# A fourth usual pair in the first gated block, statistics of later blocks made in its pairs, and rows split a pair later

## The chip, the cores and the metric

The kernel runs on one core of one Trainium2 chip. The metric is device time in microseconds (us), the median over several runs. The engines are PE (TensorE: matrix products, with its weight loads listed as PEld), DVE (VectorE), ACT (ScalarE), POOL (GpSimd) and SP (SyncE, which here only issues DMAs). Each engine takes its instructions in the order in which the program gives them.

## The reference

Four layers in a row on x of shape (1, 2048, 448), all in float32: attention, gated, attention, gated. Both attention layers share their weights, and so do both gated ones.

```python
def A(x, wqkv, wo):                      # 16 heads of 28
    q, k, v = heads_of(x @ wqkv)
    return merged(softmax(q @ k.T * 28 ** -0.5) @ v) @ wo
def B(x, w_gate, w_up, w_down):          # F = 1792
    return (sigmoid(x @ w_gate) * (x @ w_up)) @ w_down
x = x + A(layernorm(x)); x = x + B(layernorm(x))
x = x + A(layernorm(x)); x = x + B(layernorm(x))
```

## The kernel before

**Stages.** The program is written as one long order by hand: what is recorded first on an engine runs first there. A layer here means one attention layer and the gated layer after it, so there are two. Each goes through the projection (`project`), the attention (`attend`), the output projection (`out_project`) and the gated part (`gated`). x stays in SBUF all the time.

**Precision.** Matrix operands are kept as a high and a low float16 part, and a product is made of three matmuls (high-high, low-high, high-low). An ACT copy makes the high part, a DVE subtraction the low one.

**Attention.** Scores for three key tiles at a time go to three PSUM banks, and one ACT instruction (L1144) takes the exponential of all three. `FEW` says how many of a head's 64 units (a key tile by a block of queries) are taken out of this and done on DVE instead, in ten operations (L1154 to L1163, `score_aside`); the counts hold for layer 0 alone, layer 1 uses three in every head. While layer 0's attention runs, DVE and POOL also prepare the gated weights (`Prepare`): sums and splits, packed and written to DRAM.

**The gated part.** 2048 rows are four blocks b of 512 rows, and the 1792 features are seven pairs p of 256. "b1p4" is block 1, pair 4. `gate_and_up` makes one pair for one block. It uses a scheme with seven products instead of eight for 2x2 blocked matrices (Strassen's, in Winograd's form): `first`, `second`, `third` are chains whose PSUM bank ACT copies out (L1527), `c11_c22`, `c21` and `c12` complete the four quarters. DVE adds the bank `side` to the copies (L1543 after `c11_c22`, L1550 after `c12`). `c12` writes into the same `side` bank that L1543 reads. Then come the sigmoid (ACT, L1554) and the product (DVE, L1557). The order of PE in a pair is fixed: `first`, `apart`, `second`, `apart`, `third`, `c11_c22`, `c21`, `c12`, each for gate and up, at six or five matmuls of 256 columns a time.

**Down projection.** For most pairs it too has seven products: `Operands.early` and `late` make sums on DVE, `parts` and `rest` split them into `hparts` in the next pair, and while block b runs its gate and up, PE makes the products (`pieces`, L1454) of block b-1, one product k a pair, over all the pairs of that block; `finish` adds the result to x (L1472). The first `USUAL` pairs of block 0 do it the usual way instead: `split` makes one float16 pair a tile (L210, L211), and `down` runs 24 matmuls of 448 columns (L1502 to L1504) into four banks, one pair later. `add_usual(j)` adds bank j to x.

**The rest beside it.** `at[0]` to `at[5]` are lists of work recorded at six places of a pair: after `first`, `second`, `third`, `c11_c22`, the first sigmoids and products, and the end. `portions(b, p)` says how many steps of the next block's preparation are recorded at which of them. A block's 18 steps are: four `norm` (statistics of one tile of 128 rows: DVE L279 and L280, POOL L283 and L285), four `squares` (scaling L288 and a transpose L305 into `xs`), one step that stores `xs` to DRAM (SP, L317) and gathers it turned into `raw` (SP, L325 and L327), and nine that split it (`r11`, `t1`, `t2`, `t3`, `r21`, `t4`, `r22`, `last_low`, `last_rows`; DVE L371, L387, L390 and ACT L379, L381, L394).

**Slots.** Large tiles (`xn`, `xs`, `xraw`, `gu`, `dn` and others) share 19 slots of SBUF, handed out first freed, first used. When a pair is done, its two `gu` tiles (the gate weights and the up weights of a pair) are freed, and POOL issues the loads for the pair after next into the two slots that have been free longest (`used_gu`, L1345); products' weights `dn` follow (L1357). A load waits until the former holder of its slot is done, and everything behind it in POOL's queue waits too.

Of the kernel before, what the change touches and what calls it, by code (L numbers as in the profile page):

```python
# [11 lines left out]
F32 = mybir.dt.float32  # L12
BF16 = mybir.dt.bfloat16
F16 = mybir.dt.float16
# [5 lines left out]
P = 128  # L20
# [6 lines left out]
NB = 4  # L27
TB = NT // NB
# [8 lines left out]
NP = NF // 2  # L37
# [18 lines left out]

N_SUMS = 25
DN = D // 2
N_DN = 8
USUAL = 3  # L60
SHORT = ((10, 23, 12), (11, 24, 13), (8, 22, 9))

ASIDE = {1: ((6, 15, 1),), 2: ((4, 10, 3), (9, 15, 1)), 3: ((4, 9, 3), (8, 13, 1), (12, 15, 2))}
FEW = "2221212111111233"


TAIL = (0, 1, 3, 2, 5, 4, 6)
# [41 lines left out]
def interleaved_layers(ctx: ExitStack, tc: tile.TileContext, x_in, wqkv, wo, w_gate, w_up,  # L111
# [4 lines left out]
    cpool = ctx.enter_context(tc.tile_pool(name="cpool", bufs=1))  # L116
# [3 lines left out]
    big = Slots(spool, "s", N_SLOTS)  # L120
    qrt = Slots(spool, "q", N_QUART)
    uid = [0]
# [132 lines left out]
    class Block:  # L255
# [15 lines left out]
        def norm(self, js=range(TB)):  # L271
            b = self.b
            if js[0] == 0:
                uid[0] += 1
                self.mv = cpool.tile([P, TB, 2], F32, name=f"mv_{uid[0]}", tag="mv", bufs=2)
                self.rs = cpool.tile([P, TB], F32, name=f"rs_{uid[0]}", tag="rs", bufs=2)
            for j in js:
                st = cpool.tile([P, 6], F32, name=f"st_{uid[0]}_{j}", tag="st", bufs=4)
                nc.vector.bn_stats(st, x[:, b * TB + j, :])  # L279
                nc.vector.bn_aggr(self.mv[:, j, :], st)  # L280
            c = slice(js[0], js[-1] + 1)
            rs = self.rs[:, c]
            nc.gpsimd.tensor_scalar(rs, self.mv[:, c, 1], EPS, XS ** -2, op0=ALU.add,  # L283
                                    op1=ALU.mult)
            nc.gpsimd.tensor_tensor(rs, rs, nhalf[:, c], op=ALU.pow)  # L285
# [166 lines left out]

        def begin(self):
            uid[0] += 1
            self.mv = cpool.tile([P, TB, 2], F32, name=f"mv_{uid[0]}", tag="mv", bufs=2)
            self.rs = cpool.tile([P, TB], F32, name=f"rs_{uid[0]}", tag="rs", bufs=2)
            self.xn = big.get("xn", [P, TB, D])

        def stats(self, j):
# [103 lines left out]
    gu_parts = dpool.tile([NP, 2, P, N_SUMS, P], F16, name="gu_parts")  # L563
    dn_parts = dpool.tile([N_DN, P, NP, 2, DN], F16, name="dn_parts")

# [346 lines left out]
    class Prepare:  # L912
# [127 lines left out]
        def split(self, raw, kind, j):  # L1040
# [287 lines left out]
    class WeightsGated:  # L1328
# [24 lines left out]
                    nc.sync.dma_start(self.usual[p // 2][:, p % 2, i], dn_parts[k, :, p])  # L1353

        def load_dn(self, queue=nc.sync):
            self.dn.append(big.get("dn", [P, NP, 2, DN], F16))
            queue.dma_start(self.dn[-1], dn_parts[self.products.popleft()])  # L1357

        def used_gu(self):
            big.put(*self.gu.popleft())  # L1360
# [8 lines left out]
    def gated(layer, first, wt, before_next):  # L1369
        last = layer == LAYERS - 1  # L1370
# [1 line left out]
        low, high = slice(0, W // 2), slice(W // 2, W)  # L1372

        seq = [(b, p) for b in range(NB) for p in range(NP)]
        blks = [first]
        steps = deque()
        banks_of = {}


# [127 lines left out]
        def add_usual(j):  # L1507
            v = x[:, j, :]
            pm = accs[j].rearrange("p c n -> p (c n)")
            nc.vector.scalar_tensor_tensor(v, pm, back[:, 2:3], v, op0=ALU.mult, op1=ALU.add)  # L1510
# [95 lines left out]
        pend = []  # L1606
        for b, p in seq:
            if p == 0:
                if b + 1 < NB:
                    blks.append(Block(b + 1, True))  # L1610
                    steps.extend(blks[b + 1].steps())
                elif not last:
                    after = [Block(0), Block(1)]
                    blks.append(after[0])
                    steps.extend(after[0].steps())
                    ready = [steps.pop() for _ in range(2)]
                    squared = after[1].squared()
                    steps.extend(squared[:TB] + ready[::-1] + squared[TB:] +
                                 [after[1].store, after[1].gather])
            at = [[] for _ in range(6)]  # L1620

            if made:
                at[0].append(made.parts)
                at[1].append(made.rest)
            if done:
                at[1].append(lambda done=done: finish(*done))
                done = None
            for i, n in enumerate(portions(b, p)):
                at[i].append(lambda n=n: run_fill(steps, n))
            if b == 0 and p > USUAL or b == 1 and p == 0:  # L1630
                for j in range(TB)[p - USUAL - 1:p - USUAL] if b == 0 else range(
                        NP - USUAL - 1, TB):
                    at[0].append(lambda j=j: add_usual(j))


            if b > 0:
                some = [q for q in (0, 1, 6, 2, 3, 4, 5) if q in of_block(b - 1)]
                for q in some:
# [24 lines left out]

        b = NB - 1
# [10 lines left out]
        for k in TAIL[3:]:  # L1675
            if k == 6:
                for j, i in enumerate((0, 2)):
# [4 lines left out]
                    if last:  # L1682
                        t = b * TB + j
# [10 lines left out]
    def portions(b, p):  # L1694

        if b == 0:
            steps = {0: {1: 4, 5: 5}, 2: {1: 1, 2: 1, 3: 1, 5: 1}, 3: {1: 1, 2: 1, 3: 1, 5: 1},
                     4: {1: 1}}
        elif b < NB - 1:
            steps = {0: {1: 2, 2: 1}, 1: {1: 2, 2: 1}, 2: {1: 1, 2: 2}, 3: {5: 1},  # L1700
                     4: {1: 1, 3: 1}, 5: {1: 1, 3: 1}, 6: {1: 1, 2: 1, 3: 1, 5: 1}}
        else:
            steps = {0: {1: 2, 2: 1}, 1: {1: 2, 2: 1}, 2: {1: 1, 2: 2}, 3: {1: 2, 2: 2},
                     4: {1: 1, 2: 1}, 5: {1: 1, 2: 1}, 6: {1: 1, 2: 2, 5: 1}}
        return [steps.get(p, {}).get(i, 0) for i in range(6)]
# [6 lines left out]
    first = Block(0)  # L1712
# [81 lines left out]
```

## Time and profile before

| what | value |
|---|---|
| device time, median of 3 runs | 1914.47 us |
| lowest and highest | 1913.83, 1914.67 us |
| the profiled execution | 1918.24 us |
| its span, first to last instruction | 1916.4 us |
| PE busy | 1897.9 us (99%) |
| DVE busy | 1412.8 us (74%) |
| ACT busy | 1366.0 us (71%) |
| POOL busy | 240.6 us (13%) |
| granted PE clock, mean | 0.997 |

A row of the timeline gives the start in us from the span's start, the length, the engine, the line of the kernel, the operation with what it writes and reads, and how many such were merged; in brackets stands how long the engine sat idle before it and what ended that. A row of the windows view gives a stretch, its length, and for each engine the busy time in it with the number of instructions, then the mean granted clock of PE as a share of full speed. The page counts a matmul from its issue to its modelled end, and matmuls overlap, so that PE's busy time says when PE was not idle and not how fast it was.

### The profile page before, as it was taken

The numbers are of one execution on the slowest core, as the hardware profiler recorded it, in microseconds if no ns is written. First come the engines' busy times: TensorE is split into PE (matmuls) and PEld (weight loads), VectorE is DVE, ScalarE is ACT, GpSimd is POOL, SyncE is SP. The second block draws the span as 40 slices with busy tenths as digits, with TensorE's granted clock in tenths as the row PEclk, the third lists the DMA queues.
The fourth block names the chain that finished last, engine by engine and source line by source line (L and its number), as shares of the span: only waits on it lengthen the run. The fifth ranks groups of instructions, "written<-read, shape, count | busy, mean of one in ns | idle before, by whom it ended". The sixth has DMA issues, their size and how long they took to land. (4 is left out here: it accounts for less than half of the span.)

```text
span 1916.4 us, 56353 instructions
## 1 busy us (share of the span) xinstructions
PE 1897.9 (99%) x24317; PEld 1405.8 (73%) x24317; DVE 1412.8 (74%) x2816; ACT 1366.0 (71%) x1742; POOL 240.6 (13%) x467
## 2 busy tenths in 40 slices
PE   9999999999999999999999999999999999999999
PEld 4455655555566798999954568778888777899998
DVE  7648798687877598788663487778778667887764
ACT  5569999999983455454344799999999645555541
POOL 2013312232001111212100000000000011211110
PEclk9999999999999999999999999999999999999999
DMA  5575555345313657656634312122111235665752
GB/s 173 165 207 162 155 157 149 117 144 149 92 62 92 235 189 263 219 221 236 232 94 132 89 51 51 28 51 51 41 37 66 75 98 215 216 270 198 270 204 90
DMA packets 107298, 275.20 MB, mean 144 GB/s; under 512 B 12766, under 2 KB 63086, under 8 KB 106912
## 3 DMA queue, kind: packets, MB, share of 16 engines
q0 software_dynamic: 33088, 165.74, 24.5%
q1 hardware_dynamic: 73616, 105.54, 19.3%
q8 instruction: 192, 3.15, 0.7%
q14 instruction: 66, 0.54, 0.1%
q10 hardware_dynamic: 336, 0.23, 0.0%
HBM read 213.39 MB, written 50.73 MB: 138 GB/s over the span
## 5 line engine op out<-in xcount | busy, mean ns | idle before, releaser
L1144 ACT ACTIVATE prob_s<-sc 128x1536 f32<-128x1536 f32 x659 | 892.7, 1484 | 6.7 <-PE sc L1129 3.3
L1180 PE MATMUL acc<-prob_s,val_s 128*32 128x256 f32 (+3 forms) x7754 | 590.1, 383 | 0.0
L1129 PE MATMUL sc<-qp_s 114*32 114x512 f16 x7896 | 575.8, 379 | 0.0
L545 PEld LDWEIGHTS <-gu_s 128*128 128x128 f16 x4368 | 428.0, 98 | 60.3 <-issue 8.1
L1129 PEld LDWEIGHTS <-qp_s 114*32 114x32 f16 x8192 | 309.9, 96 | 176.3 <-issue 78.2
L1180 PEld LDWEIGHTS acc<-prob_s,val_s 128*32 128x32 f32 x7754 | 317.9, 110 | 100.8 <-issue 7.6
L545 PE MATMUL chain<-xwide_s,gu_s 128*128 128x256 f16 x2016 | 249.0, 273 | 4.1 <-DMA gu_s<-gu_parts 4.0
L1454 PE MATMUL dnp<-dn_s,hparts_s 128*128 128x224 f16 x2100 | 235.5, 259 | 0.0
L1454 PEld LDWEIGHTS <-hparts_s 128*128 128x128 f16 x2100 | 202.1, 98 | 4.8
L1527 ACT COPY one_q<-chain 128x256 f32<-128x256 f32 x224 | 82.0, 372 | 132.0 <-PE chain L545 131.3
L1160 DVE SCALAR_TENSOR_TENSOR power_q<-power_q,expo_q 128x512 f32<-128x512 f32 x222 | 153.7, 692 | 7.6
L545 PE MATMUL side<-xshort_s,gu_s 128*128 128x256 f16 x1120 | 142.1, 274 | 3.0 <-DVE one_q L1543 2.7
L530 PE MATMUL qkp<-xhl_s,wqk_s 128*128 128x512 f16 x616 | 138.0, 379 | 0.7 <-DVE xhl_s L509 0.3
L1543 DVE TENSOR_TENSOR one_q<-side,one_q 128x512 f32<-128x512 f32 x112 | 72.0, 684 | 83.4 <-PE side L545 83.4
L530 PEld LDWEIGHTS <-wqk_s 128*128 128x128 f16 x616 | 60.0, 98 | 70.1 <-ACT wqk_s L223 1.0
L1209 DVE STREAM_TRANSPOSE oturned_q<-acc 128x512 f32<-128x512 f32 x32 | 22.9, 717 | 118.4 <-PE acc L1180 118.4
L1345 POOL DMA_DIRECT2D gu_s<-gu_parts x104 | 56.0, 540 | 365.7 <-PE side L545 183.3
L545 PE MATMUL side<-xwide_s,gu_s 128*128 128x256 f16 x672 | 92.3, 274 | 0.0
L1407 ACT CAST hparts_s<-hsums_q 128x256 f16<-128x256 f32 (+1 forms) x144 | 68.4, 489 | 33.1 <-DVE hsums_q L1419 20.6
L722 ACT ACTIVATE qkhl_q<-qkp 128x512 f16<-128x512 f32 x56 | 33.2, 593 | 75.0 <-PE qkp L530 71.6
L1180 PE MATMUL acc<-power_q,val_s 128*32 128x256 f32 (+3 forms) x278 | 86.4, 393 | 0.0
L1554 ACT ACTIVATE one_q<-one_q 128x512 f32<-128x512 f32 x56 | 35.3, 630 | 71.3 <-DVE one_q L1543 71.2
(209 smaller groups left out, 2291.0 us busy)
## 6 DMA issues: line engine op xcount, KB each, us to landing
gu_s<-gu_parts POOLq DMA_DIRECT2D x104, 800.0 KB, 6.0
dn_s<-dn_parts POOLq DMA_DIRECT2D x50, 784.0 KB, 7.2
qp_s<-qk_scr SPq DMA_DIRECT2D x96, 224.0 KB
qk_scr<-qkhl_q SPq DMA_DIRECT2D x56, 256.0 KB
gu_parts<-pack_s POOLq DMA_DIRECT2D x14, 800.0 KB, 4.2
xt_scr<-xs_s SPq DMA_DIRECT2D x48, 224.0 KB
xraw_s<-xt_scr SPq DMA_DIRECT2D x12, 768.0 KB
qp_s<-qk_scr SPq DMA_DIRECT2D x64, 112.0 KB
```

The lines of the kernel that those rows point to most:

```text
L530: nc.tensor.matmul(pm, w, x, start=(i == 0), stop=(i == len(terms) - 1))
L545: nc.tensor.matmul(pm, a, x, start=(first and i == 0), stop=(i == len(terms) - 1), skip_group_check=True)
L1129: nc.tensor.matmul(ps[32 * j:32 * j + 32, :], hd.k[:, keys], hd.q[:, qb * W:(qb + 1) * W], start=True, stop=True, tile_position=(0, 32 * j))
L1144: nc.scalar.activation(prob[:, 0:n, :], ps[:, 0:n, :], AF.Exp, scale=exp_scale)
L1160: nc.vector.scalar_tensor_tensor(p, p, c[k], y, op0=ALU.add, op1=ALU.mult)
L1180: nc.tensor.matmul(acc[qb * VC:(qb + 1) * VC, s], v[:, kc % TB, h, :], probs[c * NB + qb][:, s], start=(kc == 0 and a == 0), stop=(kc == N ...
L1345: queue.dma_start(self.gu[-1][m], gu_parts[p, m])
L1407: nc.scalar.copy(to[:, :, 0], a)
L1454: nc.tensor.matmul(pm, a[:, x, t], w[:, p, y], start=(begin and n == 0 and (j == 0 or alone)), stop=(n == 2), skip_group_check=True)
L1527: nc.scalar.copy(to, pm)
L1543: nc.vector.tensor_tensor(one[m], side[m], one[m], op=ALU.add)
L1554: nc.scalar.activation(out, v, AF.Sigmoid, scale=gate_scale)
```

## The change

- `USUAL` goes from 3 to 4: block 0's pair 3 also goes the usual way, and block 0's products cover three pairs (4, 5 and 6) instead of four. `load_dn` leaves out the first four pairs' weights for block 0's products.
- `add_usual` for the four banks is recorded in b0p6, b1p0, b1p2 and b1p4 (`AFTER_USUAL`) instead of b0p4, b0p5, b0p6 and b1p0.
- The statistics (`norm`) of block 2 are recorded in b0p1 and those of block 3 in b0p2, two tiles after `second` and two after `third`. Those of block 1 stay in b0p0. The tiles `mv` and `rs` get four buffers each.
- Blocks 1 and 2 have 14 steps instead of 18 for the block after them. Two `squares` stand in pair 0, the other two and the store and gather in pair 1 (before: in pair 2). The split begins in pair 3.
- In block 0 the first split step, `r11`, is recorded at the end of pair 2 (before: after `second` in pair 2), and the others follow in pairs 3 to 5.
- `FEW` gives head 0 three units on DVE instead of two, and head 3 two instead of one.

```diff
+AFTER_USUAL = ((0, 6), (1, 0), (1, 2), (1, 4))
-USUAL = 3
+USUAL = 4
-FEW = "2221212111111233"
+FEW = "3222212111111233"
...
-                self.mv = cpool.tile([P, TB, 2], F32, name=f"mv_{uid[0]}", tag="mv", bufs=2)
-                self.rs = cpool.tile([P, TB], F32, name=f"rs_{uid[0]}", tag="rs", bufs=2)
+                self.mv = cpool.tile([P, TB, 2], F32, name=f"mv_{uid[0]}", tag="mv", bufs=4)
+                self.rs = cpool.tile([P, TB], F32, name=f"rs_{uid[0]}", tag="rs", bufs=4)
...
         def load_dn(self, queue=nc.sync):
-            self.dn.append(big.get("dn", [P, NP, 2, DN], F16))
-            queue.dma_start(self.dn[-1], dn_parts[self.products.popleft()])
+            t = big.get("dn", [P, NP, 2, DN], F16)
+            first = USUAL if len(self.products) > NP * (NB - 1) else 0
+            queue.dma_start(t[:, first:], dn_parts[self.products.popleft(), :, first:])
+            self.dn.append(t)
...
-        blks = [first]
-        steps = deque()
+        blks = [first] + [Block(b, True) for b in range(1, NB)]
+        steps = deque(blks[1].steps())
...
             if p == 0:
-                if b + 1 < NB:
-                    blks.append(Block(b + 1, True))
-                    steps.extend(blks[b + 1].steps())
-                elif not last:
+                assert b == 0 or not steps
+                if 0 < b < NB - 1:
+                    steps.extend(blks[b + 1].steps()[TB:])
+                elif b == NB - 1 and not last:
...
-            if b == 0 and p > USUAL or b == 1 and p == 0:
-                for j in range(TB)[p - USUAL - 1:p - USUAL] if b == 0 else range(
-                        NP - USUAL - 1, TB):
-                    at[0].append(lambda j=j: add_usual(j))
+            if (b, p) in AFTER_USUAL:
+                at[0].append(lambda j=AFTER_USUAL.index((b, p)): add_usual(j))
+            if b == 0 and p in (1, 2):
+                for i in (1, 2):
+                    at[i].append(lambda i=i: blks[1 + p].norm((2 * i - 2, 2 * i - 1)))
...
     def portions(b, p):
         if b == 0:
-            steps = {0: {1: 4, 5: 5}, 2: {1: 1, 2: 1, 3: 1, 5: 1}, 3: {1: 1, 2: 1, 3: 1, 5: 1},
-                     4: {1: 1}}
+            steps = {0: {1: 4, 5: 5}, 2: {5: 1}, 3: {1: 1, 2: 1, 3: 1, 5: 1},
+                     4: {1: 1, 2: 1, 5: 1}, 5: {1: 1}}
         elif b < NB - 1:
-            steps = {0: {1: 2, 2: 1}, 1: {1: 2, 2: 1}, 2: {1: 1, 2: 2}, 3: {5: 1},
-                     4: {1: 1, 3: 1}, 5: {1: 1, 3: 1}, 6: {1: 1, 2: 1, 3: 1, 5: 1}}
+            steps = {0: {1: 1, 2: 1}, 1: {1: 1, 2: 2}, 3: {2: 1, 5: 1}, 4: {1: 1, 5: 1},
+                     5: {1: 1, 2: 1, 5: 1}, 6: {1: 1, 3: 1}}
```

More of the change, by code (lines that the diff above doesn't have):

```diff
@@ L454, in begin @@
             uid[0] += 1
-            self.mv = cpool.tile([P, TB, 2], F32, name=f"mv_{uid[0]}", tag="mv", bufs=2)
-            self.rs = cpool.tile([P, TB], F32, name=f"rs_{uid[0]}", tag="rs", bufs=2)
+            self.mv = cpool.tile([P, TB, 2], F32, name=f"mv_{uid[0]}", tag="mv", bufs=4)
+            self.rs = cpool.tile([P, TB], F32, name=f"rs_{uid[0]}", tag="rs", bufs=4)
             self.xn = big.get("xn", [P, TB, D])
@@ L1608, in gated @@
             if p == 0:
-                if b + 1 < NB:
-                    blks.append(Block(b + 1, True))
-                    steps.extend(blks[b + 1].steps())
-                elif not last:
+                assert b == 0 or not steps
+                if 0 < b < NB - 1:
+                    steps.extend(blks[b + 1].steps()[TB:])
+                elif b == NB - 1 and not last:
                     after = [Block(0), Block(1)]
-                    blks.append(after[0])
                     steps.extend(after[0].steps())
```

## The prediction, made before the changed kernel ran

> **What bounds the kernel now.** I read the busy shares of the profile's page first, then the busy time of each engine pair by pair (the windows view), then the timeline around every pair that is longer than its neighbours. TensorE (PE) is busy 99% of the span, so only PE's own work and PE's few waits count.
>
> ```profile
> span 1916.4 us, 56353 instructions
> PE 1897.9 (99%) x24317; PEld 1405.8 (73%) x24317; DVE 1412.8 (74%) x2816; ACT 1366.0 (71%) x1742; POOL 240.6 (13%) x467
> L1144 ACT ACTIVATE prob_s<-sc 128x1536 f32<-128x1536 f32 x659 | 892.7, 1484 | 6.7 <-PE sc L1129 3.3
> ```
>
> The third row is the softmax exponential: 659 ACT instructions, only 6.7 us of idle before them, so ACT sets the pace in attention. The gated part is different. Below are windows, one a pair of F-tiles: length, then busy us of PE, weight load, DVE, ACT, POOL, then the granted clock. In order: layer 0, block 0, pairs 1 to 4 (b0p1 to b0p4); b1p0 to b1p4; b2p0; then layer 1's b0p2, b0p3, b1p1, b1p4.
>
> ```profile
> core 0: us, PE busy (x) PEld busy (x) DVE busy (x) ACT busy (x) POOL busy (x), PEclk, DMA share, GB/s
> 614.28:627.55 13.27, 13.21 (x104) 9.97 (x102) 11.03 (x22) 5.99 (x14) 0.55 (x1) 1.00 0.60 169
> 627.55:645.69 18.14, 14.80 (x103) 10.57 (x102) 9.75 (x22) 6.74 (x16) 2.60 (x6) 0.91 0.42 146
> 645.69:658.75 13.06, 13.06 (x104) 9.98 (x103) 7.46 (x19) 7.55 (x20) 0.38 (x1) 1.00 0.80 299
> 658.75:667.26 8.51, 8.51 (x79) 7.62 (x78) 4.87 (x12) 4.79 (x14) 1.15 (x3) 1.00 0.76 309
> 684.31:695.19 10.88, 10.88 (x105) 9.90 (x103) 10.42 (x27) 5.92 (x17) 4.26 (x10) 1.00 0.26 82
> 695.19:706.35 11.16, 11.02 (x104) 9.90 (x102) 10.55 (x23) 5.29 (x13) 2.39 (x6) 1.00 0.79 287
> 706.35:717.17 10.82, 10.82 (x105) 9.95 (x103) 10.24 (x23) 5.53 (x14) 1.05 (x2) 1.00 0.63 183
> 717.17:727.98 10.81, 10.81 (x104) 9.93 (x103) 8.05 (x18) 6.15 (x15) 2.11 (x4) 1.00 0.74 243
> 727.98:740.95 12.97, 10.99 (x105) 9.87 (x104) 10.05 (x23) 6.35 (x16) 1.59 (x3) 1.00 0.75 293
> 762.58:775.12 12.54, 12.54 (x123) 11.66 (x122) 10.55 (x25) 6.94 (x18) 3.84 (x9) 1.00 0.74 279
> 1571.97:1590.12 18.15, 15.11 (x104) 10.51 (x103) 9.76 (x22) 6.73 (x16) 2.89 (x6) 0.91 0.43 150
> 1590.12:1603.17 13.05, 13.05 (x103) 9.99 (x102) 7.44 (x18) 7.54 (x20) 0.04 (x1) 1.00 0.74 292
> 1639.61:1650.78 11.17, 11.03 (x104) 9.91 (x103) 10.55 (x23) 5.28 (x13) 2.40 (x6) 1.00 0.77 289
> 1672.41:1687.12 14.71, 12.65 (x104) 10.72 (x103) 10.04 (x23) 6.35 (x16) 1.59 (x3) 0.88 0.67 262
> ```
>
> A pair without down products takes 8.51 us, with a usual pair's 24 down matmuls 13.06, with 24 product matmuls of block 0 10.82, with 42 12.54. Two pairs a layer are long: b0p2 (18.14 for 13.06; layer 1 18.15 for 13.05) and b1p4 (12.97 for 10.82; layer 1 14.71), and b1p1 by a little (11.16, 11.17). Their causes:
>
> ```profile
> 635.49 0.76 DVE L371 TENSOR_TENSOR t_q<-xraw_s 128x256 f32<-128x256 f32 x2 [9.55 <-DMA xraw_s<-xt_scr]
> 636.59 1.25 PE L545 MATMUL chain<-xshort_s,gu_s 128*128 128x256 f16 x10 [2.55 <-ACT one_q L1527]
> 638.64 2.29 PE L545 MATMUL side<-xshort_s,gu_s 128*128 128x256 f16 x10 [0.79 <-DVE one_q L1543]
> 713.70 2.31 SPq L317 DMA_DIRECT2D xt_scr<-xs_s  x4
> 723.27 0.38 SPq L325 DMA_DIRECT2D xraw_s<-xt_scr  x1
> 723.70 0.53 POOL L1345 DMA_DIRECT2D gu_s<-gu_parts  x1 [9.20 <-DMA xt_scr<-xs_s]
> 726.75 1.08 POOL L1345 DMA_DIRECT2D gu_s<-gu_parts  x2 [2.00 <-PE side L545]
> 730.78 0.83 PE L545 MATMUL chain<-xwide_s,gu_s 128*128 128x256 f16 x6 [1.98 <-DMA gu_s<-gu_parts]
> 731.44 0.82 PE L545 MATMUL side<-xwide_s,gu_s 128*128 128x256 f16 x6
> 1675.29 0.99 PE L545 MATMUL chain<-xwide_s,gu_s 128*128 128x256 f16 x6 [2.06 <-DMA gu_s<-gu_parts]
> 1677.35 2.40 PE L545 MATMUL chain<-xwide_s,gu_s 128*128 128x256 f16 x12
> ```
>
> In b0p2 the split of the next block's rows (r11) stands in `along(1)`, its rows have not landed until 635.49, and DVE and ACT wait in order with the pair's own copies behind them. In b1p4 the second gate/up weight tile lies in the slot that the next block's `xs` held: the store leaves SP at 713.70, has landed at 723.27, POOL issues the load at 723.70, and PE goes on at 730.78.
>
> **Removed.** Both stalls and the small one, if nothing comes in their place: 5.08 + 5.10 + 0.34 + 0.35 + 2.15 + 3.89 = 16.9 us. r11 moves to the end of b0p2: DVE reaches it near 640 at the earliest (the pair starts no sooner than 627.55 and its gate and up matmuls take 8.5), 4 us after 635.49; the 24 down matmuls (4.55) then cover what follows. I cost the moved splits in block 0 at nothing on that cover. Without it the 5.1 us would stay.
>
> **PE work.** A fourth usual pair adds 13.06 - 8.51 = 4.55 us to block 0; block 1 loses 42 product matmuls, 12.54 - 8.51 = 4.03, or 0.58 a pair. Net +0.52 a layer, +1.0 in all. Pairs of block 1 then take 10.24 instead of 10.82.
>
> **Two units to VectorE.** Two of three banks of one exponential: 892.7/659 = 1.355, so 0.9 us less ACT in layer 0, which ACT paces. The bounds are 0 (PE becomes late) and 0.9; I take -0.9. DVE, busy 74% of the span, has room there. The eighth product of pair 3's weights (two more small DVE operations and a larger DMA) lies in the same room: nothing. So are the four more small `usual` DMAs on SP, issued in the output projection and used five pairs later, and the product loads of block 0, which only get smaller.
>
> **Statistics in b0p1 and b0p2.** Here I see a new wait. Rows of b0p1, then of b1p0 to b1p2:
>
> ```profile
> 620.31 0.68 DVE L211 TENSOR_TENSOR hhl_q<-two_q,hhl_q 128x512 f16<-128x512 f32 x1
> 620.91 1.28 DVE L1543 TENSOR_TENSOR one_q<-side,one_q 128x512 f32<-128x512 f32 x2
> 621.92 1.26 PE L545 MATMUL side<-xshort_s,gu_s 128*128 128x256 f16 x10
> 689.96 0.62 DVE L279 BATCH_NORM_STATS2 st<-x 128x6 f32<-128x448 f32 x1
> 692.17 1.27 DVE L1543 TENSOR_TENSOR one_q<-side,one_q 128x512 f32<-128x512 f32 x2
> 692.90 1.30 PE L545 MATMUL side<-xshort_s,gu_s 128*128 128x256 f16 x10
> 703.36 1.25 DVE L1543 TENSOR_TENSOR one_q<-side,one_q 128x512 f32<-128x512 f32 x2
> 704.06 1.30 PE L545 MATMUL side<-xshort_s,gu_s 128*128 128x256 f16 x10
> 711.41 0.50 DVE L288 TENSOR_SCALAR xn_s<-x,mv,rs 128x448 f32<-128x448 f32 x1
> 713.59 1.25 DVE L1543 TENSOR_TENSOR one_q<-side,one_q 128x512 f32<-128x512 f32 x2
> 1702.36 12.20 SPq L1477 DMA_DIRECT2D out_dram<-x  x4
> ```
>
> In b0p1 DVE comes out of the four `squares` and the low halves (L211) straight into `c11_c22` (L1543, 620.91), which is already late; PE's last products `c12` (the `side` group at 621.92) overwrite that bank and must wait for it. How close they follow shows later: 692.17 to 692.90 and 703.36 to 704.06, 0.7 us. The change puts four row tiles of statistics of block 2 ahead of this L1543. Three took 692.17 - 689.96 = 2.21, so four 2.95: L1543 at 623.86, `c12` at 624.57, 2.65 late, with its second half 2.7. Nothing covers it, since `c12` heads PE's queue with the down matmuls behind it. Bounds: 0 if DVE were free sooner, 3.0 if all of it counts. In b0p2 DVE has the time of the down matmuls for block 3's four: nothing. POOL's rs operations there stand ahead of no load that is due.
>
> **Block 1, two layers alike.** b1p0: three statistics leave (2.21), two `squares` come (713.59 - 711.41 = 2.18), so L1543 stays at 692.14 and `c12` at 692.85, 8.54 after the pair's start; but with one product less ahead PE is there at 8.0. Stall 0.6, with the second half 0.65; b1p1 0.1. Later DVE has 8.05 us of its own work a pair (717.17 row) against 10.24. b1p4 and b1p5 add `add_usual` and splits of 2.5 to 3.2: about 0.3 together, bounds 0 and 1.5.
>
> The store moves to b1p1, and with it the slot: the load that takes it is now the second tile of b1p3, again two pairs on. Before, the store left 713.70 - 706.35 = 7.35 after the pair's start, and PE went on 17.08 later. DVE reaches the end of the last two `squares` at 7.3 in b1p1 as well (the statistics that stood before them left). So the tile is there 24.5 after b1p1's start, and wanted after 10.34 + 10.24 + 0.66 = 21.2 (0.66: the first tile's six matmuls, 731.44 - 730.78): a stall of 3.3, more than the 2.15 of before, because the pairs in between are shorter. Bounds: 0.3 (the two transfers quicker by 3) and 6. In block 2 the two pairs take 25.1, so the same 24.5 is hidden. On SP the store passes nothing in block 1; in layer 1's block 2 the output DMAs stand before it, the last issued by 1714.6, and b2p1 begins near 1721 (1672.41 + 14.71 + 2 x 10.82 + 12.54). On POOL the loads due later stand behind the waiting load (rival 1).
>
> New waits a layer: 2.7 + 0.65 + 0.1 + 3.3 + 0.3 = 7.05, 14.1 in all.
>
> **The clock.** The same wait in b1p4 cost layer 1 14.71 - 12.97 = 1.74 more: after 1675.29 the clock falls (0.88 in its window) and twelve matmuls take 2.40, where six took 0.82 (731.44). In layer 0 it did not fall. In b0p2 it fell in both layers (0.91). So three of four waits over 2 us were followed by 1.7 us; the new kernel has four again, 2.7 and 3.3 long. I take three: +5.1, bounds 0 and 6.8.
>
> [...]
>
> **Sum:** -16.9 + 1.0 - 0.9 + 14.1 + 5.1 = +2.4 us. The profiled execution took 1918.24 us (span 1916.4), 3.8 above the runs' median of 1914.47, and I carry the difference over: 1916.9. No slow stretch gives 1911.8, four 1918.6.
>
> **Rivals.** (1) Slower: the b1p3 load itself is held up. POOL now issues block 0's next product and both tiles of b1p4 right behind it, their slots being free; before, those two waited until 726.75. If they share the way with it and it takes 10 us instead of 7.1, each layer loses 2.9: +8, 1922.7. It decides once the load takes over 9 us. Against: a product load stood right behind it before, too. 0.15. (2) The statistics cost nothing, because `c12` doesn't wait for L1543: -5.4 and the 2.6 of their slow stretches, 1909. Against: the 0.79 at 638.64 names L1543. 0.09. (3) The earlier store and load meet emptier queues (smaller product loads) and take 3 us less: -6 and -3, 1908. 0.08. (4) No slow stretch follows the new waits, as none followed 730.78: 1911.8. 0.05. [...] (5) The r11 stall stays, because the rows land later than 640: up to +10, 1927. 0.03.
>
> **Numbers.** The forecast has 0.60: 1911.8 to 1918.6, with 1.5 more either side. 0.2% is 3.8 us, about what a measurement here tells from no change. Of the forecast a third lies above +3.8, almost none below -3.8. Slower: 0.20 + 0.15 + 0.03 = 0.38. Faster: rivals 2 and 3 and a little of the rest, 0.18. Within: 0.44. The range, 1908.5 to 1922.0, leaves out rivals 5, half of 1 and 3, and tails.
>
> **What would show it.** Right: b0p2 at 13.1, b0p1 near 16 with PE's `side` group idle on DVE one_q before it; b1p4 at about 10.5 and b1p3 at 13.5 to 15.3 with the wait on gu; block 2 unchanged at 12.54; one exponential fewer (658). Wrong: b0p1 at 13.3, b1p3 near 10.3, or r11 still waiting for `xraw`.

## The result, and the profile after

| what | before | after |
|---|---|---|
| device time, median of 5 runs on one chip | 1914.67 us | 1922.74 us |
| lowest and highest | 1913.83, 1915.91 us | 1921.67, 1925.29 us |
| ratio to before, 95% interval | | 1.0043, 1.0028 to 1.0058 |
| the profiled execution | 1918.24 us | 1921.67 us |
| predicted | | 1916.9 us, 1908.5 to 1922.0 |

The change makes the kernel 0.43% slower, 8.1 us. The prediction said +2.4 us. Most of the mechanisms that it named came, and four terms of its sum were off. The two profiled executions differ by only 3.4 us, so the first thing to explain is why the runs differ by more than the traces.

The page of the changed kernel: PE is idle for 22.9 us, 4.4 us more than before, of a span that is 3.6 us longer.

```profile
span 1920.0 us, 56172 instructions
PE 1897.1 (99%) x24233; PEld 1315.1 (68%) x24233; DVE 1420.7 (74%) x2820; ACT 1361.6 (71%) x1731; POOL 235.7 (12%) x451
```

Its windows, with the columns of the prediction's windows. In order: layer 0's b0p1, b0p2, b0p4, b1p0, b1p3, b1p4, b1p5, b1p6; layer 1's b0p1 and b1p3.

```profile
613.92:629.88 15.96, 13.42 (x104) 9.97 (x102) 15.12 (x34) 5.99 (x14) 2.90 (x6) 1.00 0.49 140
629.88:642.94 13.06, 13.06 (x103) 9.99 (x102) 8.20 (x20) 5.19 (x13) 3.44 (x8) 1.00 0.89 323
656.00:669.05 13.05, 13.05 (x103) 9.97 (x102) 7.68 (x20) 6.94 (x18) 0.47 (x1) 1.00 0.52 198
686.09:696.92 10.83, 10.46 (x98) 9.34 (x96) 10.40 (x25) 5.92 (x17) 2.05 (x4) 1.00 0.43 156
717.40:732.62 15.22, 12.08 (x98) 10.07 (x97) 8.43 (x20) 6.18 (x16) 1.06 (x2) 0.89 0.59 224
732.62:743.33 10.71, 10.45 (x99) 9.35 (x97) 10.20 (x24) 6.28 (x15) 0.54 (x1) 1.00 0.48 186
743.33:753.96 10.63, 10.59 (x99) 9.35 (x97) 10.12 (x23) 6.95 (x17) 2.94 (x6) 1.00 0.48 183
753.96:764.98 11.02, 10.40 (x99) 9.37 (x98) 9.51 (x22) 7.37 (x19) 2.28 (x5) 1.00 0.89 341
1560.93:1578.59 17.66, 15.11 (x105) 10.42 (x102) 16.62 (x38) 5.99 (x14) 4.43 (x10) 0.90 0.55 156
1666.10:1679.62 13.52, 10.41 (x98) 9.27 (x97) 8.43 (x20) 6.17 (x16) 1.06 (x2) 1.00 0.68 257
```

b0p2 is down from 18.14 to 13.06 as foreseen, and the fourth usual pair has the length it should (13.05). b0p1 has grown from 13.27 to 15.96, b1p3 from 10.81 to 15.22, and b1p4, b1p5 and b1p6 stand at 10.71, 10.63 and 11.02 where 10.24 is the length without a wait. In two windows the clock is at 0.89 and 0.90: b1p3 of layer 0 and b0p1 of layer 1 hold a half-clock stretch each, their twins in the other layer none. (A half-clock stretch is some 3.4 us in which the granted clock is at 0.50, in b1p3 from 722.6 to 726.0; each of the five in the two profiles, of before and after, is that long. It costs 1.7 us: PE is busy for 12.08 us there and for 10.41 in the twin.) The timeline shows the causes, three in order:

```profile
620.55 0.62 DVE L281 BATCH_NORM_STATS2 st<-x 128x6 f32<-128x448 f32 x1
623.48 1.27 DVE L1547 TENSOR_TENSOR one_q<-side,one_q 128x512 f32<-128x512 f32 x2
624.21 1.30 PE L547 MATMUL side<-xshort_s,gu_s 128*128 128x256 f16 x10 [2.48 <-DVE one_q L1547]
...
704.26 2.32 SPq L319 DMA_DIRECT2D xt_scr<-xs_s  x4
713.73 0.38 SPq L327 DMA_DIRECT2D xraw_s<-xt_scr  x1
714.13 0.53 POOL L1347 DMA_DIRECT2D gu_s<-gu_parts  x1 [9.07 <-DMA xt_scr<-xs_s]
721.36 0.83 PE L547 MATMUL chain<-xwide_s,gu_s 128*128 128x256 f16 x6 [3.14 <-DMA gu_s<-gu_parts]
...
755.67 0.71 ACT L381 CAST xshort_s<-xraw_s 128x256 f16<-128x256 f32 x2
756.29 0.64 ACT L1531 COPY one_q<-chain 128x256 f32<-128x256 f32 x2
756.70 1.47 PE L547 MATMUL chain<-xwide_s,gu_s 128*128 128x256 f16 x12 [0.62 <-ACT one_q L1531]
```

First b0p1: DVE makes four tiles of statistics from 620.55 to 623.48, `c11_c22` (L1547 here) follows, and PE's `side` products have waited 2.48 us for it. Then b1p3: the store leaves SP at 704.26, has landed by 713.73, POOL's load goes out at 714.13, and PE, ready for the second tile after 717.40 + 0.66, starts it at 721.36. Last b1p6, which the prediction did not see: a copy of the next block's split (L381), recorded at the end of b1p5, stands in ACT's queue ahead of the `one` copies (L1531), and PE waits for those to free the bank.

### The profile page after: what moved, and what is told of

Read it like the earlier page. It is cut to its first block, busy times and chain, and to the rows that moved or that the text cites. A ratio compares the mean times of both kernels' runs of the same rounds, so it can differ in the third digit from the quotient of the medians.

```text
span 1920.0 us, 56172 instructions
## 1 busy us (share of the span) xinstructions
PE 1897.1 (99%) x24233; PEld 1315.1 (68%) x24233; DVE 1420.7 (74%) x2820; ACT 1361.6 (71%) x1731; POOL 235.7 (12%) x451
## 5 line engine op out<-in xcount | busy, mean ns | idle before, releaser
L1182 PE MATMUL acc<-prob_s,val_s 128*32 128x256 f32 (+3 forms) x7700 | 568.6, 384 | 0.0
L1131 PE MATMUL sc<-qp_s 114*32 114x512 f16 x7888 | 552.6, 379 | 0.0
L1131 PEld LDWEIGHTS <-qp_s 114*32 114x32 f16 x8192 | 265.1, 95 | 218.2 <-issue 104.1
L1182 PEld LDWEIGHTS acc<-prob_s,val_s 128*32 128x32 f32 x7700 | 267.9, 110 | 144.8 <-issue 10.4
L1458 PE MATMUL dnp<-dn_s,hparts_s 128*128 128x224 f16 x2016 | 225.2, 259 | 0.0
L1458 PEld LDWEIGHTS <-hparts_s 128*128 128x128 f16 x2016 | 194.0, 98 | 4.4
L1531 ACT COPY one_q<-chain 128x256 f32<-128x256 f32 x224 | 82.2, 372 | 143.1 <-PE chain L547 142.3
L1162 DVE SCALAR_TENSOR_TENSOR power_q<-power_q,expo_q 128x512 f32<-128x512 f32 x228 | 157.8, 692 | 7.8
L1547 DVE TENSOR_TENSOR one_q<-side,one_q 128x512 f32<-128x512 f32 x112 | 71.9, 684 | 98.4 <-PE side L547 98.4
L1211 DVE STREAM_TRANSPOSE oturned_q<-acc 128x512 f32<-128x512 f32 x32 | 22.9, 716 | 119.2 <-PE acc L1182 119.1
L1182 PE MATMUL acc<-power_q,val_s 128*32 128x384 f32 (+3 forms) x284 | 88.7, 394 | 1.1 <-issue 1.1
```

Source lines behind the costliest of these rows:

```text
L1131: nc.tensor.matmul(ps[32 * j:32 * j + 32, :], hd.k[:, keys], hd.q[:, qb * W:(qb + 1) * W], start=True, stop=True, tile_position=(0, 32 * j))
L1162: nc.vector.scalar_tensor_tensor(p, p, c[k], y, op0=ALU.add, op1=ALU.mult)
L1182: nc.tensor.matmul(acc[qb * VC:(qb + 1) * VC, s], v[:, kc % TB, h, :], probs[c * NB + qb][:, s], start=(kc == 0 and a == 0), stop=(kc == N ...
L1458: nc.tensor.matmul(pm, a[:, x, t], w[:, p, y], start=(begin and n == 0 and (j == 0 or alone)), stop=(n == 2), skip_group_check=True)
L1531: nc.scalar.copy(to, pm)
L1547: nc.vector.tensor_tensor(one[m], side[m], one[m], op=ALU.add)
```

## Experiments

Every run is set against runs of the kernel before on the same chip at the same time (medians 1915.49 us for runs 1 to 4, 1914.68 for 5 to 8, 1914.99 for 9 to 12). The mean granted clock of each run helps to count the half-clock stretches: one stretch of 3.4 us at half clock lowers the mean over the span by 0.0009, and the profiles agree (one stretch counted at 0.999, two at 0.998, three at 0.997, four at 0.996). Counts per run below are estimates made so, and since the clock is recorded in steps of 0.001, the count of a single run is good to about half a stretch. Runs with the same clock still differ, by up to 4.4 us (26 runs of the kernel before at 0.999: 1912.53 to 1916.93). Part of that lies ahead of the gated blocks: in the five windows shown here of b0p1 of layer 0, of kernels that are alike up to there, it starts between 613.03 and 615.91 us.

**1. The kernel before again, unchanged.**

> The kernel before, unchanged. Two theories of the 5 us that the sum missed. Theory A (profiled execution not typical): the profiled execution of before held more half-clock stretches (three, of 1.7 us) than most executions of it, so its 1918.24 us lie 3.6 above the median of its runs, and the difference that the change makes has to be taken from a typical trace. Then this profile shows none or one such stretch (b0p2 near 16.5 us instead of 18.1 in the layers where it is missing) and a time within 2 us of the median of its own runs, 1914 to 1916. Theory B (constant offset): the profile adds some 3.6 us to every execution of this kernel. Then this profile again has three stretches or so and 1917.5 to 1919 us, while the runs stay at 1914 to 1915.

Its profile took 1913.07 us, the runs 1913.07 to 1917.62 (median 1915.95). Windows of b0p2 and b1p4, layer 0 and then layer 1:

```profile
627.07:644.55 17.48, 14.89 (x104) 10.71 (x102) 8.98 (x21) 6.73 (x16) 1.83 (x4) 0.90 0.44 152
726.83:740.00 13.17, 10.98 (x104) 9.84 (x102) 10.04 (x23) 6.34 (x16) 1.58 (x3) 1.00 0.77 300
1570.39:1586.60 16.21, 13.43 (x104) 9.95 (x102) 8.38 (x20) 6.73 (x16) 1.35 (x3) 1.00 0.45 163
1668.88:1682.04 13.16, 10.99 (x105) 9.84 (x103) 10.05 (x23) 6.39 (x16) 1.58 (x3) 1.00 0.77 297
```

One stretch, in b0p2 of layer 0, where the first profile had three. The two b0p2 pairs take 17.48 and 16.21 instead of 18.14 and 18.15, and b1p4 of layer 1 13.16 instead of 14.71. Theory A holds, though this profile lies further below its median (2.9 us) than it said: 1918.24 was a long execution, not one with a constant offset. The 27 runs of the same kernel beside it go from 1912.33 to 1919.55, and over 70 runs of it (59 beside the experiments and these 11) the median is 1915.4 and the mean count 2.2 stretches.

**2 to 4. The two new waits, one at a time and together.**

```diff
-            if b == 0 and p in (1, 2):
+            if b == 0 and p == 2:
                 for i in (1, 2):
-                    at[i].append(lambda i=i: blks[1 + p].norm((2 * i - 2, 2 * i - 1)))
+                    at[i].append(lambda i=i: blks[1 + i].norm())
```

> The changed kernel, with the statistics of blocks 2 and 3 both in b0p2 (eight tiles, four after second and four after third), none in b0p1. If the statistics ahead of the c11_c22 addition in b0p1 are what holds PE's c12 up for 2.65 us: b0p1 at 13.3 in both layers, -5.3 us, and with 0 to 2 half-clock stretches gone -5.3 to -8.7; 1914 to 1917.4 us against the changed kernel's median of 1922.7. If b0p2 has no room for eight tiles, its length grows from 13.05 by up to 2.5 a layer and the gain is 0 to 3. If the wait of b0p1 is not from the statistics: 1922.7.

```diff
         # store
-            big.put(xs)
+            if not self.halves:
+                big.put(xs)
         # r11
+                if not self.turned:
+                    big.put(self.xs)
```

> The changed kernel, with the slot of xs of blocks 1 to 3 given back when r11 is recorded instead of when the store is recorded, so that the second gate/up tile of b1p3 takes a slot that PE left at the end of b1p1 and doesn't wait for the store. If the store is what makes the tile 3.3 us late: b1p3 at 10.3, -6.6 us, and with 0 to 2 half-clock stretches gone -6.6 to -10; 1912.7 to 1916.1 us against 1922.7. If the way of the load itself is late (POOL's queue, or transfers that share it), b1p3 keeps 1 to 3.3 us of its wait and the time is 1918 to 1922.7.

> The two edits of the second and third run together. Theory A (the new waits and the half-clock stretches that follow them are the whole price of the change): -11.9 us for the waits and -3.4 to -6.8 for two to four stretches, 1904 to 1907.4 us, the profile without any stretch in blocks 0 and 1, and runs that lie within 1.5 us of each other, where those of the changed kernel spread over 3.6. Theory B (the change costs something else besides, some 5 us that the trace doesn't show): 1909 to 1912, with the same spread as before.

Measured: 1917.23 us for the statistics (ratio 1.0006, 0.9997 to 1.0015), 1917.19 for the slot (1.0009, 1.0000 to 1.0018), 1908.82 for both (0.9966, 0.9952 to 0.9979), against 1.0043 for the change as it was. By the differences of the ratios times 1915 us that is -7.1, -6.5 and -14.7 us, nearly additive. The second run is at the end of its range, the third between its two theories. Windows of the second run's b0p1, b0p2 and b1p3 in layer 0, then of the third run's b1p3:

```profile
615.91:629.18 13.27, 13.22 (x105) 9.97 (x103) 12.58 (x27) 5.99 (x14) 0.54 (x1) 1.00 0.58 166
629.18:642.23 13.05, 13.05 (x103) 9.99 (x102) 10.74 (x27) 5.20 (x13) 4.60 (x8) 1.00 0.80 292
716.69:731.59 14.90, 11.78 (x99) 9.98 (x97) 8.43 (x20) 6.18 (x16) 1.06 (x2) 0.89 0.60 234
716.65:728.16 11.51, 10.44 (x98) 9.33 (x96) 7.76 (x18) 6.08 (x15) 1.05 (x2) 1.00 0.53 184
```

b0p1 is back at 13.27, and b0p2 takes all eight tiles at no cost (13.05), so the statistics in b0p1 were that wait. With the slot freed later b1p3 is at 11.51 instead of 15.22. The fourth run's windows of b1p3 and b1p4, and then, from its timeline, DVE's row in b1p3:

```profile
714.31:725.70 11.39, 10.45 (x99) 9.34 (x98) 7.77 (x18) 6.09 (x15) 1.05 (x2) 1.00 0.56 187
725.70:736.98 11.28, 10.58 (x98) 9.34 (x97) 10.76 (x25) 6.32 (x15) 0.54 (x1) 1.00 0.46 173
```

```profile
721.99 0.76 DVE L374 TENSOR_TENSOR t_q<-xraw_s 128x256 f32<-128x256 f32 x2 [3.12 <-DMA xraw_s<-xt_scr]
```

The wait for the tile is gone, and what was behind it comes out: DVE stands for 3.12 us at the split's first step, because the gathered rows land only at 721.99, and b1p3 keeps 1.1 us (0.6 in layer 1). So the store was the cause, as the first theory of the third run says, with a remainder that neither had. The fourth run's runs spread over 2.3 us (1906.68 to 1908.97), four of five at a clock of 1.000: with the waits the stretches went too. Theory A misses by 1.4 to 4.8 us; 1.1 and 0.6 of it are these waits, and b1p4 is 0.6 longer than in the changed kernel (11.28 for 10.71) in either layer, 2.9 in all. Theory B's time nearly came (1908.82 against 1909 to 1912), its spread did not, and what the trace shows accounts for the time.

**5. The changed kernel again.**

> The changed kernel, unchanged. Theory A (the waits of its trace are there in every execution, 2.65 us in b0p1 and 3.3 us in b1p3 of each layer, and only the number of half-clock stretches behind them varies): the same four waits within 0.1 us in this profile, its time near 1918.3 us plus 1.7 for each stretch counted in it (the first profile had two and took 1921.67), and a median of the runs of 1922 to 1924 with the kernel before at 1914.5 to 1915.5. Theory B (the waits themselves vary as those of the kernel before did): waits that differ by 0.5 us or more from 2.65 and 3.3.

Median 1923.40, ratio 1.0043 (1.0027 to 1.0059), profile 1922.35. b0p1 and b1p3 of layer 0, then of layer 1:

```profile
614.81:630.78 15.97, 13.43 (x104) 9.95 (x102) 15.13 (x34) 5.99 (x14) 3.12 (x7) 1.00 0.52 149
718.30:733.58 15.28, 12.08 (x98) 10.12 (x96) 8.42 (x20) 6.17 (x16) 1.06 (x2) 0.89 0.58 225
1561.87:1579.52 17.65, 15.10 (x104) 10.45 (x102) 16.62 (x38) 5.99 (x14) 4.42 (x10) 0.90 0.51 144
1667.04:1680.30 13.26, 10.42 (x99) 9.27 (x97) 8.43 (x20) 6.18 (x16) 1.06 (x2) 1.00 0.67 259
```

The same waits (2.7 us twice; 3.4 and 3.0 against 3.3 twice), again two stretches in the profile, and by the clocks of the eleven runs of this kernel (five with the result and these six) 3.3 stretches a run. That is theory A, but the load's wait varies more than it said (in the profile of run 6 it is some 3.7 in both layers). Neither profile of this kernel has a stretch behind b1p3's wait in layer 1.

**6 and 10. Two units less on VectorE,** once on the changed kernel and once on the ninth run's (below).

```diff
-FEW = "3222212111111233"
+FEW = "2221212111111233"
```

> The changed kernel with the old counts of units on VectorE (head 0 two, head 3 one). If two units are worth 0.9 us of ACT, as the prediction had it: 0.9 us slower than the changed kernel, 1923.6 against 1922.7, and 334 exponentials instead of 332 rows in layer 0. If PE becomes late where the units stand (the profile of the changed kernel shows ACT idle for 1.0 us at head 0's units): the same time as the changed kernel, within 0.5 us.

> The kernel of the ninth run with the old counts of units on VectorE. If the two units are worth 0.9 us: 0.9 us slower than the ninth run. If ACT waits in layer 0's attention for as long as the two units save: within 0.5 us of it. (With the four waits and their half-clock stretches away, the runs should lie close enough to tell the two apart.)

1925.75 us against 1923.40 in the first place (ratios 1.0050 and 1.0043, intervals of 0.0016 either side: not to be told apart; by the clocks it had 4.1 stretches a run for 3.3, which is 1.3 us of it). In the second all ten runs lie within 0.6 us: 1902.36 (1902.26 to 1902.79) against 1902.37 (1902.19 to 1902.65). The two units are worth 0.0. The groups of exponentials in layer 0's projection and attention, first with the two units (the ninth run), then without:

```profile
L1149 ACT ACTIVATE prob_s<-sc 128x1536 f32<-128x1536 f32 x332 | 447.9, 1516 | 4.7 <-PE sc L1134 4.5
```

```profile
L1149 ACT ACTIVATE prob_s<-sc 128x1536 f32<-128x1536 f32 x332 | 447.5, 1518 | 3.7 <-PE sc L1134 3.2 <-DMA qp_s<-qk_scr 0.3
L1149 ACT ACTIVATE prob_s<-sc 128x1024 f32<-128x1024 f32 x1 | 1.1, 1054 | 0.0
```

The exponential of 1.1 us is saved, but ACT waits 4.7 us instead of 3.7, and the 332 others take 0.4 longer: nothing is left. By the traces of the kernel before and the changed kernel, which have the counts of runs 10 and 9, 3.1 us of either wait stand ahead of the first exponential, and the 1.0 more is one wait for PE's scores, beside a unit that is done on DVE: the changed kernel has it at 199.40, and the kernel before, without the two units, has none there, only 0.33 us after the third exponential.

```profile
199.40 369.49 ACT L1146 ACTIVATE prob_s<-sc 128x1536 f32<-128x1536 f32 x274 [1.02 <-PE sc L1131]
```

**7. The split moved alone,** on the kernel before.

```diff
-            steps = {0: {1: 4, 5: 5}, 2: {1: 1, 2: 1, 3: 1, 5: 1}, 3: {1: 1, 2: 1, 3: 1, 5: 1},
-                     4: {1: 1}}
+            steps = {0: {1: 4, 5: 5}, 2: {5: 1}, 3: {1: 1, 2: 1, 3: 1, 5: 1},
+                     4: {1: 1, 2: 1, 5: 1}, 5: {1: 1}}
```

> The kernel before with only the split of block 1's rows moved, as the change has it (r11 at the end of b0p2, the others in pairs 3 to 5); three usual pairs, statistics and block 1 as before. If the waits of b0p2 were all there was to win and nothing takes their place: b0p2 at 13.06 in both layers instead of 16.2 to 18.1, -6.3 to -10.2 us, 1905 to 1909 us against 1915.5. If the split steps, now in b0p4 and b0p5 without a usual pair's 24 matmuls as cover, hold up the additions there: b0p4 and b0p5 longer than 8.51 by 0.5 to 1.5 each, 1 to 3 us a layer given back, 1907 to 1912.

1910.48 us, ratio 0.9976 (0.9966 to 0.9987). Windows of layer 0's b0p2, b0p5 and b0p6, then rows of the timeline around the waits in the last two:

```profile
626.92:639.98 13.06, 13.06 (x104) 9.97 (x102) 6.71 (x15) 5.19 (x13) 2.13 (x4) 1.00 0.78 292
661.55:670.71 9.16, 8.70 (x80) 7.62 (x78) 8.57 (x23) 6.60 (x20) 1.68 (x4) 1.00 0.42 150
670.71:680.41 9.70, 8.69 (x80) 7.54 (x78) 7.86 (x20) 5.80 (x18) 1.08 (x3) 1.00 0.72 285
```

```profile
664.16 1.47 PE L545 MATMUL chain<-xwide_s,gu_s 128*128 128x256 f16 x12 [0.46 <-ACT one_q L1527]
665.70 1.60 POOL L1345 DMA_DIRECT2D gu_s<-gu_parts  x3 [15.14 <-ACT two_q L1527]
672.54 0.83 PE L545 MATMUL chain<-xwide_s,gu_s 128*128 128x256 f16 x6 [1.01 <-DMA gu_s<-gu_parts]
```

b0p2 is at 13.06, and 1.8 us are given back in layer 0, in b0p5 and b0p6 rather than b0p4 and b0p5: once by ACT's copies, late behind the split's, and once by a gate/up load that POOL issued only at 665.70, after 15.14 us without work, so that it landed 1.01 us late. In the changed kernel the fourth usual pair lies over these steps, and b0p5 and b0p6 have no wait (8.52 each). So that pair, which costs 0.5 us of PE a layer, probably covers these 1.8 as well. No run shows this by itself, since the changed kernel also has fewer additions of usual banks in these two pairs.

**8 and 9. The remaining waits,** on the kernel of run 4. (`...` in the lists stands for entries that stay as they are.)

```diff
-AFTER_USUAL = ((0, 6), (1, 0), (1, 2), (1, 4))
+AFTER_USUAL = ((0, 5), (0, 6), (1, 2), (1, 3))
...
-            steps = {..., 3: {2: 1, 5: 1}, 4: {1: 1, 5: 1}, 5: {1: 1, 2: 1, 5: 1}, 6: {1: 1, 3: 1}}
+            steps = {..., 3: {5: 1}, 4: {1: 1, 3: 1}, 5: {3: 2}, 6: {3: 2, 5: 2}}           # run 8
+            steps = {..., 3: {5: 1}, 4: {1: 1, 3: 1}, 5: {1: 1, 3: 1},                      # run 9
+                     6: {1: 1, 2: 1, 3: 1, 5: 1}}
```

> The fourth run's kernel (statistics later, slot freed later) with the split in block 1 moved behind the landing of its rows (r11 at the end of pair 3, two steps a pair after that, the last four at the end of pair 6) and the additions of the usual banks in b0p5, b0p6, b1p2 and b1p3. The fourth run still showed waits of 0.54 (b1p0), 0.6 to 1.1 (b1p3, DVE waiting for the gathered rows), 0.87 with 0.14 (b1p4), 0.35 (b1p5) and 0.78 us (b1p6) in each layer, 3.5 a layer. If DVE's room in a pair is what matters and it is now kept: block 1's pairs at 10.24 to 10.3 throughout, -6 to -7 us, 1902 to 1903 us against 1908.8. If the work only moves its wait elsewhere (b0p5, b0p6 or the start of block 2): 1905 to 1909.

The eighth run took 1916.16 us, 7 more than the fourth instead of 6 less. Its windows of b1p4, b1p6 and b2p0 in layer 0 and of b2p0 in layer 1, and then two rows of the timeline in layer 0's b2p0:

```profile
724.18:734.42 10.24, 10.24 (x99) 9.36 (x97) 9.82 (x24) 6.74 (x17) 1.60 (x3) 1.00 0.52 194
744.91:756.42 11.51, 10.86 (x99) 9.33 (x98) 8.68 (x20) 6.74 (x17) 1.18 (x3) 1.00 0.55 214
756.42:771.71 15.29, 12.78 (x120) 11.55 (x120) 13.20 (x29) 8.11 (x20) 3.15 (x6) 1.00 0.55 215
1699.84:1716.87 17.03, 14.52 (x121) 12.54 (x121) 13.27 (x30) 8.11 (x20) 3.15 (x6) 0.90 0.58 221
```

```profile
760.93 0.40 ACT L397 COPY xshort_s<-xshort_s 64x256 f16<-64x256 f16 x1 [1.46 <-DVE xshort_s L390]
761.78 1.47 PE L550 MATMUL chain<-xwide_s,gu_s 128*128 128x256 f16 x12 [2.51 <-ACT one_q L1534]
```

Block 1's pairs 0 to 4 are at 10.24, so DVE's room was judged right. But the last two steps, at the end of b1p6, put a copy that waits for DVE (L397, 760.93) ahead of ACT's `one` copies of the next pair, and PE waits 2.51 us for those, in layer 1 with a stretch behind it.

> The eighth run's kernel with the split in pairs 5 and 6 of blocks 1 and 2 recorded as the kernel before has it (one step after second and one after c11_c22 in pair 5; in pair 6 one after second, third, c11_c22 and at the end). The eighth run had block 1's pairs 0 to 4 at 10.24 us, but lost 1.3 us in b1p6 and 4 us at the start of blocks 2 and 3, where the last steps stood ahead of ACT's copies of the next pair. If those two steps at the end of pair 6 are the cause: b2p0 at 12.54, b1p5 and b1p6 10.24 to 10.8, 1901 to 1904 us. If DVE's room is short anyway: b1p5 and b1p6 each 0.5 to 1 us over 10.24, 1904 to 1908.

The ninth run took 1902.37 us (1902.19 to 1902.65), ratio 0.9937 (0.9923 to 0.9950), 12.6 us under the kernel before and 20 under the change. Its windows of b1p0, b1p3, b1p5, b1p6 and b2p0 in layer 0:

```profile
683.61:693.86 10.25, 10.25 (x99) 9.35 (x97) 9.82 (x24) 5.91 (x17) 2.04 (x4) 1.00 0.46 164
714.34:724.58 10.24, 10.24 (x99) 9.35 (x97) 8.26 (x19) 5.60 (x14) 1.05 (x2) 1.00 0.60 206
734.82:745.31 10.49, 10.49 (x99) 9.34 (x97) 10.05 (x22) 6.53 (x17) 1.89 (x4) 1.00 0.62 234
745.31:755.55 10.24, 10.24 (x99) 9.37 (x97) 9.45 (x22) 7.43 (x18) 1.66 (x4) 1.00 0.61 239
755.55:768.09 12.54, 12.54 (x123) 11.66 (x121) 11.13 (x25) 7.28 (x18) 2.01 (x4) 1.00 0.68 262
```

Of these only b1p5 is above its length, by 0.25. All five runs have a clock of 1.000.

**11 and 12. How long a wait has to be.** The ninth run's kernel, with the statistics of three or two of block 2's tiles put back into b0p1.

```diff
+            if b == 0 and p == 1:                       # run 11
+                at[1].append(lambda: blks[2].norm((0, 1)))
+                at[2].append(lambda: blks[2].norm((2,)))
...
+            if b == 0 and p == 1:                       # run 12
+                at[2].append(lambda: blks[2].norm((0, 1)))
```

> The kernel of the ninth run with the statistics of three of block 2's four tiles back in b0p1 (the other five tiles in b0p2). The wait of c12 in b0p1 was 2.65 us with four tiles; a tile is 0.74, so 1.9 us with three, in each layer: +3.8 us. Theory A (a half-clock stretch becomes the likelier the longer the wait is: 2.1 us waits were followed by one in about 4 of 10 cases, 2.65 us in about 8 of 10, 3.3 us always): 0.3 to 0.8 stretches a run, +0.5 to +1.4 us, in all +4.3 to +5.2. Theory B (only the number of waits counts): 1.6 or more stretches a run, in all +6.5 or more. [...]

> The kernel of the ninth run with the statistics of two of block 2's tiles back in b0p1, after third (the other six in b0p2). A wait of 2.65 - 2 x 0.74 = 1.2 us in each layer: +2.4 us. Theory A: hardly any stretch, the clocks of the runs at 1.0 or 0.999, in all +2.4 to +2.8. Theory B (only the number of waits counts): +5 or more.

1905.84 us (+3.5) and 1904.38 (+2.0); the windows of b0p1 in layer 0:

```profile
613.34:628.59 15.25, 13.43 (x104) 9.95 (x102) 14.45 (x32) 5.99 (x14) 3.71 (x9) 1.00 0.64 198
```

```profile
613.03:627.54 14.51, 13.42 (x104) 9.95 (x102) 13.75 (x30) 5.99 (x14) 2.53 (x5) 1.00 0.62 189
```

15.25 and 14.51 instead of 13.27, so waits of 1.98 (layer 1's b0p1 takes 15.25 too) and 1.24. All ten runs have a clock of 1.000: not one stretch behind twenty waits (two a run, with layer 1 of run 12 taken to be as layer 0). So the eleventh run pays for its waits alone (+3.5 measured, +3.8 expected for them), and the twelfth has the clocks that theory A says. Theory B falls (+6.5 or more, +5 or more). Theory A is weakened and not excluded: at its low end it expects 1.5 stretches in the five runs of the eleventh, and there is none. (Two of the twelfth's runs, 1906.47 and 1907.14, lie 2 to 3 us above the others at the same clock, a spread that the kernel before has too; no trace of these two shows why.)

## Why the prediction was wrong

**Right.** r11's move brings b0p2 to 13.06 (predicted 13.1), and in the changed kernel at no cost where the steps went. The fourth usual pair costs what was said (13.05 for 8.51, and 10.24 in block 1). One exponential fewer is counted (658). c12's wait in b0p1 is 2.7 (2.7), b1p0's 0.59 (0.65), b1p3's 3.3 in both layers (3.3), by the chain of store, load and slot that was worked out; block 2 is unchanged. None of the rivals came: the time is that of rival 1, but the load that it speaks of was not held up (a wait of 3.3 and not 6.2 us), and stretches do follow waits of this length (1 of 2 in b0p1 and 1 of 2 in b1p3 of the changed kernel's first profile), against rival 4.

**Wrong, four terms.** The largest error is in the new waits, then comes the number of half-clock stretches, then the two units, then the waits removed. Waits below leave out the half-clock stretches, which are counted apart.

| term | predicted | measured | difference |
|---|---|---|---|
| waits removed | -11.8 | -11.3 (run 1) | +0.5 |
| two units on VectorE | -0.9 | 0.0 (run 10) | +0.9 |
| new waits, both layers | +14.1 | +16.4 | +2.3 |
| half-clock stretches, 1.7 us each | 3 gone, 3 new | some 2.2 gone, 3.3 new | +1.9 |
| fourth usual pair | +1.0 | +1.0 | 0 |
| sum | +2.4 | +8.0 | +5.6 |

The runs gave +8.1. (16.4 is, a layer, 2.70 + 0.59 + 3.3 + 0.47 + 0.39 + 0.78; 11.3 is, from the first run's windows, 17.48 - 13.05 - 1.7 and 16.21 - 13.05 in b0p2 and 13.17 + 13.16 - 2 x 10.82 in b1p4, and 0.34 + 0.35 in b1p1, which is from the prediction's trace.) As a check on all terms but that of the stretches, runs with the same clock: at 0.997 the kernel before took 1917.2 in the mean of 15 runs and the changed one 1923.5 in the mean of 7, 6.3 apart, where -11.3 + 0.0 + 16.4 + 1.0 gives 6.1. And the ninth run, which has neither the old waits nor the new and no stretch: -11.3 - 2.2 x 1.7 + 1.0 + 2 x 0.25 = -13.5 us (with layer 1's b1p5 taken to be as layer 0's), measured -12.6 by the medians and -12.1 by the ratio, so about 1 us stays open. The waits removed are read from one trace, and the counts of stretches are estimates: agreement to some tenths of a us is partly luck.

- **The step "b1p4 and b1p5 add `add_usual` and splits ... about 0.3 together"** was the mis-sized wait: 0.86 in these two, and b1p6 was left out. The step counted DVE's work a pair, and DVE was indeed short (10.20 busy of 10.71). It did not look at ACT, where the split's copy at the end of a pair stands ahead of the next pair's copies that free a PSUM bank: 0.78 more. Runs 8 and 9 show both sides: room for DVE alone gave 10.24 up to b1p4, and then the same ACT queue took it back until the steps were put after `second` and later.
- **"I take -0.9"** counted ACT's work and not whether PE's scores keep up; the bound 0 was named, and was the answer.
- **"I carry the difference over"** hid part of this. Of the 3.8 us that the profiled execution of before took above the median, 1.0 was the median, which came from three runs (1914.47; 1915.4 over 70); about 1.4 was its three stretches where its runs have 2.2 in the mean; the rest lies within the spread of runs with the same clock. To carry the 3.8 over supposes that the changed kernel's runs lie as far below a trace with three stretches; but it has 3.3 stretches a run, and its two medians lie 1.1 us above its two profiles instead. The sum cancelled three stretches against three, where by the clocks a run of the changed kernel has one more than a run of the kernel before (3.3 and 2.2). From trace to trace the sum was off by only 1.0 us, because the changed kernel's first profile had one stretch less than the sum and longer waits than it.

## What to carry to other kernels

When a profiled execution differs from the median of its runs, find out first what is different in it (here the clock of each run told how many half-clock stretches it had) before its terms are added up. A wait of PE had two prices here, its length and the chance of half the clock behind it (1.7 us), so two waits of 1.2 us (not one of ten was followed by a stretch) can cost less than one of 2.7 (6 of 10 traced ones were). And a step that is moved has to be looked at on each queue that it uses: the last split steps had room on DVE and cost 0.8 to 2.7 us by ACT, where they stood ahead of the next pair's first copies.

## What the runs showed of the hardware

A half-clock stretch followed some waits of PE in these runs and not others, and the longer waits far more often. In the profiled executions a stretch followed 1 of 4 waits of 2.15 to 2.35 us (b1p4 in the kernel before and in run 1; in run 7's profile, whose block 1 is that of the kernel before, the clock is 1.000 throughout), 6 of 10 waits of some 2.7 us (b0p1 in both profiles of the changed kernel and in runs 3 and 6, b2p0 in run 8) and 6 of 8 waits of 2.9 to 3.7 us (b1p3 in both profiles of the changed kernel and in runs 2 and 6). By the clocks of the runs, if every stretch is put down to the two longest waits of a kernel, the estimates are: none in twenty waits of 1.2 and 2.0 us (runs 11 and 12, ten runs with two waits each); 0.37 a wait in b1p4 of run 7 (12 runs), some 2.2 us if it is as long there as in the kernel before; 0.81 at 2.7 us (run 3, 11 runs); 1.0 at 3.0 us (run 2, 11 runs). The last one is too high for a single wait: two of the eight traced waits of this length, of 3.0 and 3.3 us, were not followed, and two of run 2's runs have clocks of 0.997 and 0.996, which is three and four stretches beside two long waits. Whether 3.3 us is worse than 2.7 is not shown. Nor is it shown that the length alone decides: between 2.0 us (none of ten in run 11) and some 2.2 (0.37) there is hardly a difference in length, but run 7's kernel has other waits beside these, of 0.46 and 1.01 us, and the ninth run's, to which runs 11 and 12 add theirs, is over its lengths by 0.25 us alone in the windows shown.

So gaps of some 2.7 us were followed by half the clock in most of the traced cases (6 of 10), and of the waits that were tried by themselves those of up to 2.0 us had no stretch behind them in ten runs. The same wait can be followed in one layer and not in the other: in the first profile of the changed kernel PE sits idle for 3.14 us in layer 0's b1p3, with a stretch behind it (0.89), and for 3.11 us in layer 1's, without one (1.00).
